# The last token group of a gated state-space mixer, finished in halves, with engines fixed per operation and an order made with an allowance for loads

## The chip, the cores and the metric

The kernel runs on one core of a Trainium2 chip. The metric is the device time of one launch, in microseconds. The core has a matrix engine (TensorE, PE in the profile, with its weight loads as PEld), a vector engine (VectorE, DVE), a scalar engine for tables of functions (ScalarE, ACT) and a queue engine (SyncE, SP), and sixteen DMA engines that both SyncE's and ScalarE's queues feed. Each engine works its own instructions in the order in which they were issued; what depends on another engine waits at a semaphore, and everything behind it on the same engine waits too.

## The reference, cut to what matters

The input is 2048 tokens of 512 channels. It is normalised over the channels, and two branches start from the result xn.

```python
xn = _layernorm(x, axis=-1)
s = _A_ref(xn, ...)          # a long convolution: K from (A, B, C, dt), y = irfft(rfft(K) * rfft(xn)) + xn * Dskip
g = _silu(_B_ref(xn, ...))   # the gate
return x + s * g

# _B_ref: spatial-shift token mixing, then an MLP
h = _gelu(_layernorm(x) @ w1)
hs = concat(shift(h quarters by +1, -1, +2, -2)) @ w2
x1 = x + hs
return x1 + _gelu(_layernorm(x1) @ w3) @ w4        # w3: 512 x 1376, w4: 1376 x 512
```

The convolution kernel K of a channel is a sum over 128 complex modes of a geometric sequence in the token's number. Both K and the convolution run over all 2048 tokens of a channel, so the scan branch needs all tokens before it can give any.

## The kernel before, in words

The tile X holds all tokens in the on-chip memory: 128 partitions x 16 slots x 512 channels, float32. A token group is two slots, 256 tokens; there are eight groups, worked in the order 1, 2, ..., 7, 0 (the list GROUPS). X is overwritten stage by stage: with the normalised input, with x1, with x1 plus the MLP, with its Silu (the gate), with the gate times the scan, and with the final sum.

The stages are these. *params* prepares the modes from A, B, C and dt. *token_mixing* normalises (ln_first), transposes and multiplies by w1 (h_pair, into pb), applies gelu, starts the transform of the tokens (u_stage1), and multiplies the shifted rows by w2 (hs_pair, into pd); on the way the weights w3 and w4 are scaled and split into a high and a low float16 half (prep). *tables* makes the exponentials and waves of all modes (mag, pt) and sums them into K by products into pc. *mlp* multiplies a group's rows by w3 in six blocks (into pb, waiting for x1T, which a DMA transposes), applies gelu into g, splits g into the high and low halves ghl, and accumulates ghl times w4 in pa; the last line of mlp adds the scaled pa to X. *kstage1* and *products* do the transforms of K and the product with the tokens' spectra, for each half of the channels (DH = 256 channels): eight units a half, each of which loads constants (cst), spectra (kin, uin), multiplies, and stores its result (z1e) to a scratch in device memory. *gate* applies Silu to a group, *inverse* loads the scratch (zin), transforms it back and multiplies X by it, and *finish* adds the input (xr, loaded again) and stores the group in four DMAs of 32 partitions.

The groups 1 to 7 take the inverse's result one half of the channels at a time. The last group, 0, keeps the result of both halves in pc (duo[2]) and multiplies by it once, 1024 elements a partition (lines 1238 to 1243).

Each function of ScalarE belongs to a set of tables: exponentials, sine and Silu, gelu, square root, arctangent. A change of set is an instruction of its own (ACT_TABLE_LOAD, issued at line 539).

None of this fixes the order in which instructions are issued. The program first only notes operations, 1751 of them, with what they read and write (Plan.add). Plan.order then walks through time with one clock for each engine and a cost for each operation, and issues them (Plan.issue). At each step it takes the engine that can start next, and on it, of the operations ready within 0.02 us, the one with the lowest value in the table DUE, with a charge for a change of tables (SWITCH) and for a change of TensorE's array mode (KEEP). Work that either VectorE or ScalarE can do (Either: copies, scalings) is offered to both, with a preference by engine (PREFERP, AVOIDP, PREFER, AVOID); a store can go to SyncE's or to ScalarE's queue. A transfer is counted as landed at the time done (lines 515 and 516). Since every instruction is issued by one of two lines, the profile has nearly all of them under L542 (and L539 and L541), and the names of the tiles tell them apart.

The lines that the change touches: release and the choice (464 to 491), the landing of a transfer (515), gate (1223), inverse (1227), finish (1247), mlp (1431 to 1470).

Of the kernel before, what the change touches and what calls it, by code (L numbers as in the profile page):

```python
# [21 lines left out]
D = 512  # L22
# [73 lines left out]
class Op:  # L96
# [17 lines left out]
FIRST, LAND, PAD, LANES = 1.7, 0.45, 0.13, 8  # L114
# [9 lines left out]
SHIFT, KEEP = 0.09, -41.4  # L124
# [159 lines left out]
)  # L284
SWITCH = 196.28
PREFERP, AVOIDP = 150.95, -129.56
PREFER, AVOID = -68.73, 92.63

# [48 lines left out]
class Plan:  # L337
# [115 lines left out]
    def order(self):  # L453
# [10 lines left out]
        def release(op):  # L464
            for e in op.alts:
                pools[e].append(op)
# [1092 lines left out]
```

## Time and profile before

| what | value |
|---|---|
| median of 3 runs | 549.91 us (548.17 to 551.24) |
| profiled execution | 550.05 us, span 548.3 us |
| granted TensorE clock, mean | 0.987 |
| TensorE busy | 524.2 us, 6058 products |
| VectorE busy | 443.2 us, 730 instructions |
| ScalarE busy | 401.5 us, 587 instructions, of them 51 table loads of 1.28 us |
| moved by DMA | 107.33 MB |

The span is the time from the first to the last instruction on the core; the profiled execution's own time has 1.75 us beside it. Busy is the time in which an engine works an instruction; a transfer that is issued counts for the DMA engines and not for the engine that issued it. In an answer of the trace a bracket after an instruction is the time for which its engine was idle before it, and what ended that. A group of lines "x12" is twelve instructions in a row merged.

### The profile page before, as it was taken

What the parts mean: (1) busy time and instruction counts of PE and PEld (TensorE: products, weight loads), DVE (VectorE), ACT (ScalarE), POOL (GpSimd) and SP (SyncE); (2) the same over time, 40 slices, a digit from 0 to 9 for tenths busy, and PEclk for the clock granted to TensorE, in tenths of its full rate; (3) what the DMA queues carried; (4) which work ended last, traced back from release to release, by engine and by line L of the source; (5) the groups of instructions that cost most, each with busy time, mean ns of one, the idle gap of its engine ahead of it and who ended that gap; (6) DMA issues with size and microseconds to landing.
All of it is one profiled execution on the core that took longest, in us unless ns stands there. A gap on an engine that the chain in (4) does not pass through costs nothing.

```text
span 548.3 us, 14226 instructions
## 1 busy us (share of the span) xinstructions
PE 524.2 (96%) x6058; PEld 345.9 (63%) x6058; DVE 443.2 (81%) x730; ACT 401.5 (73%) x587; POOL 0.7 (0%) x6
## 2 busy tenths in 40 slices
PE   9789999999999999899999999999999998999992
PEld 9687676876444576458567657576765666466641
DVE  5899999799999999999999989978244353874376
ACT  2899999699997999997999995968345421722511
POOL 0000000000000000000000000000000000000000
PEclk9989999999999999999999999999999999999997
DMA  8974667844666624566434344446898867969977
GB/s 209 222 192 141 232 219 240 281 138 152 217 196 248 133 59 113 141 199 182 139 122 153 96 145 131 124 135 191 213 347 290 287 193 248 280 182 233 327 248 231
DMA packets 86591, 107.33 MB, mean 196 GB/s; under 512 B 31680, under 2 KB 65728, under 8 KB 85632
## 3 DMA queue, kind: packets, MB, share of 16 engines
q1 hardware_dynamic: 85808, 104.46, 63.6%
q10 hardware_dynamic: 720, 1.97, 1.1%
q8 instruction: 47, 0.77, 0.6%
q14 instruction: 16, 0.13, 0.1%
HBM read 64.46 MB, written 37.75 MB: 186 GB/s over the span
## 4 chain that ended last, share of the span: by engine, by line
PE 71%; DVE 11%; DMA 8%; ACT 6%; issue 2%; SPq 1%; DVEq 0%; ACTq 0%
PE pb L542 29%; PE pa L542 18%; PE pd L542 13%; PE pc L542 10%; DVE X L542 3%; DVE pt L542 3%; DMA cst<-c_gp 2%; ACT mag L542 2%; DMA zin<-scr_Zdb 1%; DMA X<-in_A_u_dram 1%; SPq L542 1%; DMA rawA<-in_A_A_re_dram 1%; ACT pt L542 1%; DVE ghl L542 1%; ACT L539 1%
## 5 line engine op out<-in xcount | busy, mean ns | idle before, releaser
L542 PE MATMUL pb<-x1T,w3h 128*128 128x256 f16 (+1 forms) x1056 | 122.9, 273 | 0.4 <-DMA x1T<-x1s 0.4
L542 PE MATMUL pa<-w4h,ghl 128*128 128x512 f16 (+1 forms) x528 | 122.3, 380 | 0.2 <-DVE ghl L542 0.2
L542 PEld LDWEIGHTS <-w3h 128*128 128x128 f16 (+1 forms) x1056 | 102.8, 100 | 26.7 <-issue 10.8
L542 PEld LDWEIGHTS <-ghl 128*128 128x128 f16 (+1 forms) x528 | 49.3, 98 | 61.8 <-issue 8.7
L539 ACT ACT_TABLE_LOAD x51 | 65.4, 1283 | 8.8 <-DMA out_dram<-X 7.3
L542 ACT ACTIVATE pt<-pt 128x2048 f32<-128x2048 int32 x32 | 60.7, 1906 | 2.0 <-DVE pt L542 1.9
L542 PE MATMUL pb<-xT,w 128*128 128x256 f32 x256 | 59.1, 383 | 1.1 <-ACT xT L542 1.1
L542 DVE TENSOR_TENSOR pt<-mag,pt 128x1024 f32<-128x1024 f32 x48 | 57.5, 1217 | 1.2 <-ACT pt L542 1.1
L542 DVE SCALAR_TENSOR_TENSOR ghl<-g,wsc,ghl 128x512 f16<-128x512 f32 (+1 forms) x48 | 33.4, 701 | 30.9 <-ACT ghl L542 30.6
L542 PE MATMUL pd<-w,hT 128*128 128x512 f32 x116 | 53.1, 599 | 1.4 <-DVE X L542 1.4
L542 PEld LDWEIGHTS pb<-xT,w 128*128 128x128 f32 x256 | 47.2, 190 | 10.7 <-issue 2.7
L542 ACT ACTIVATE g<-pb,wsc 128x512 f32<-128x512 f32 (+1 forms) x48 | 30.5, 649 | 27.3 <-PE pb L542 26.3
L542 ACT ACTIVATE ghl<-g,wsc 128x512 f16<-128x512 f32 (+1 forms) x38 | 26.0, 689 | 28.1 <-PE pa L542 28.0
L542 ACT ACTIVATE mag<-par 128x128 f32<-128x128 f32 x160 | 41.0, 454 | 2.8 <-DMA is<-c_is 2.6
L542 PEld LDWEIGHTS pd<-w,hT 128*128 128x128 f32 x116 | 21.3, 190 | 27.4 <-issue 24.2
L542 DVE TENSOR_TENSOR pt<-pt 128x2048 f32<-128x2048 f32 x16 | 36.4, 2283 | 0.2 <-ACT pt L542 0.2
L542 DVE TENSOR_TENSOR pr<-pd,uin 128x1024 f32<-128x1024 f32 x16 | 19.3, 1221 | 20.3 <-PE pd L542 20.3
L542 PEld LDWEIGHTS pc<-pt 128*32 128x32 f32 x2048 | 29.7, 110 | 9.2 <-issue 8.7
L542 PE MATMUL pc<-pt 128*32 128x64 f32 x2048 | 33.0, 220 | 0.7 <-issue 0.7
L542 ACT ACTIVATE pt<-pt,halfpi 128x2048 f32<-128x2048 f32 x16 | 32.0, 2000 | 0.2
L542 ACT COPY z1e<-pc 128x1024 f32<-128x1024 f32 x7 | 7.1, 1013 | 22.6 <-PE pc L542 22.6
L542 DVE TENSOR_TENSOR pt<-par,ev 128x1024 int32<-128x1024 f32 x16 | 19.5, 1216 | 4.2 <-PE pc L542 4.2
(155 smaller groups left out, 760.2 us busy)
## 6 DMA issues: line engine op xcount, KB each, us to landing
wst<-in_B_w_dram SPq DMA_DIRECT2D x20, 512.0 KB, 4.2
scr_Ud<-ue SPq DMA_DIRECT2D x16, 512.0 KB, 3.3
uin<-scr_Ud SPq DMA_DIRECT2D x32, 256.0 KB, 4.2
cst<-c_gp SPq DMA_DIRECT2D x16, 384.0 KB, 4.6
scr_Uh<-uh SPq DMA_DIRECT2D x8, 512.0 KB, 3.4
scr_Kfa<-k1e SPq DMA_DIRECT2D x8, 512.0 KB, 3.3
kin<-scr_Kfa SPq DMA_DIRECT2D x16, 256.0 KB, 3.0
scr_Zda<-z1e SPq DMA_DIRECT2D x8, 512.0 KB, 5.6
```

Source lines behind the costliest of these rows:

```text
L539: self.engines["ACT"].preload_act_table_set(SETS[table])
L542: ins = [getattr(self.engines[op.eng], name)(*args, **kw).ins for name, args, kw in op.calls]
```

## The change

Three things change together.

First, the last token group is finished in two halves of one slot each (new function pieces). The scaled addition of pa at the end of mlp, the Silu of gate, the product of inverse, the addition of finish: each is done for one slot and then for the other, 512 elements a partition where it was 1024, and each half is stored by four DMAs of its own, eight in all. Before the scaled addition of this group, ScalarE is given a Silu of one element that reads the last gelu's result and writes a scratch element (warm), so that the table of Silu is asked for there.

Second, each operation that two engines can do has its engine fixed by a table of bits (PIN, one for each of now 1760 operations: 1 is VectorE, or SyncE for a store; 0 is ScalarE). The four preferences are gone.

Third, the order is made by other rules: an operation that isn't ready yet can be chosen too, with a charge (WAIT) for each microsecond that it would be waited for; the charges for tables and array mode have other values; the planner counts a transfer as landed MARGIN = 0.6 us later when it decides when its readers are ready (its DMA lanes are freed as before); and the table DUE is new throughout.

```diff
-FIRST, LAND, PAD, LANES = 1.7, 0.45, 0.13, 8
+FIRST, LAND, MARGIN, PAD, LANES = 1.7, 0.45, 0.6, 0.13, 8
-SHIFT, KEEP = 0.09, -41.4
+SHIFT = 0.09
...
-SWITCH = 196.28
-PREFERP, AVOIDP = 150.95, -129.56
-PREFER, AVOID = -68.73, 92.63
+SWITCH, KEEP, WAIT = 35.498, -5.69, 93.442
+PIN = (
+    "10111111111111111111111111111111111111111110111101111111100111111101101111111111111010010010010110011111111111"
...
         def release(op):
-            for e in op.alts:
-                pools[e].append(op)
+            e = min(op.alts)
+            if len(op.alts) > 1 and PIN[op.idx] == "1":
+                e = max(op.alts)
+            pools[e].append(op)
...
             for o in pools[e]:
-                if o.ready <= t + 0.02:
-                    v = o.vt
...
+                v = o.vt + WAIT * max(0.0, o.ready - t)
+                if e == "ACT" and o.table and o.table != table:
+                    v += SWITCH
+                if e == "PE" and o.mode != mode:
+                    v += KEEP
+                if pick is None or (v, o.idx) < score:
+                    pick, score = o, (v, o.idx)
+            pools[e].remove(pick)
             pick.eng = e
+            t = max(t, pick.ready)
...
                 landed.append(done)
+                done += MARGIN
...
     def gate(g):
-        X2 = X[:, 2 * g : 2 * g + 2]
-        A.activation(X2, X2, AF.Silu)
+        for x, _ in pieces(g):
+            A.activation(X[:, x], X[:, x], AF.Silu)
...
         if g == GROUPS[-1]:
             if hf == 0:
                 return
-            ch, py = slice(0, D), pair
+            for x, k in pieces(g):
+                V.tensor_mul(X[:, x], X[:, x], pair[:, k])
+            return
...
-        X2 = X[:, 2 * g : 2 * g + 2]
-        V.tensor_add(X2, X2, xr[q][:, 2 * (g % 2) : 2 * (g % 2) + 2])
-        for r in range(4):
-            E.store(ov[ORDER[r]][:, 2 * g : 2 * g + 2], X2[32 * r : 32 * r + 32])
+        for x, k in pieces(g):
+            V.tensor_add(X[:, x], X[:, x], xr[q][:, 2 * (g % 2) : 2 * (g % 2) + 2][:, k])
+            for r in range(4):
+                E.store(ov[ORDER[r]][:, x], X[32 * r : 32 * r + 32, x])
...
+    def pieces(g):
+        if g != GROUPS[-1]:
+            return [(slice(2 * g, 2 * g + 2), slice(0, 2))]
+        return [(2 * g + k, k) for k in range(2)]
...
-        X2 = X[:, 2 * g : 2 * g + 2]
-        V.scalar_tensor_tensor(X2, duo[0], a4, X2, op0=ALU.mult, op1=ALU.add)
+        if g == GROUPS[-1]:
+            A.activation(warm[:fr], g32[:fr, 0, 0:1], AF.Silu)
+        for x, k in pieces(g):
+            V.scalar_tensor_tensor(X[:, x], duo[0][:, k], a4, X[:, x], op0=ALU.mult, op1=ALU.add)
```

The values of DUE are in units of the planner's own. The ones that the prediction names are counted to their place: the first normalised rows on ScalarE have about -1605, the exponentials of the same time -360 to -280; the last products into pa have -1214 and -1236, the last scan product of group 7 has -713.

More of the change, by code (lines that the diff above doesn't have):

```diff
@@ L131 @@
 DUE = (
[152 rows of a table removed]
-)
-SWITCH = 196.28
-PREFERP, AVOIDP = 150.95, -129.56
-PREFER, AVOID = -68.73, 92.63
[142 rows of a table added]
+)
+SWITCH, KEEP, WAIT = 35.498, -5.69, 93.442
+PIN = (
+    "10111111111111111111111111111111111111111110111101111111100111111101101111111111111010010010010110011111111111"
+    "11111111100010101101101010111111111111111111111111111111111111010110110101011111111111111111111111110000111011"
+    "01101111101111110110101111111111111111111111111101111111111011011111111101101101010111111111111111111111111111"
+    "10111011011010111110111101101110111111111111110101010101010101010101011111111111111111111111111011111111111111"
+    "11111111111111111111111111111111101101111111111111111111111111111011011111111111111111111111111111111111111110"
+    "11011111111111111111111101101101111111101111101111101111101111101111101111101111101001100110100000000011111100"
+    "01111111101111111000111111111111111100011111111011111110001111111101010000000001111110001111111101111111000111"
+    "11111011111110001111111101111111000111111110111001111101111110011110110011110111111001111001111100111110011111"
+    "00111001100111101111110011110011111111001110011111011110011111111011111101111111011111101111111111111101111111"
+    "01111110111111101111110111111101111110111111101111111111111111111110101000000000111111000111111110111111100011"
+    "11111101111111000111111110111111100011111111010100000000011111100011111111011111110001111111101111111000111111"
+    "11111111110001111111101110111111001111100111101111111101111110011110011111001111100111110011100110011110011111"
+    "01111100111110111111011111100111001111111101111110011110111111011111100111110111110111011110111111011111001111"
+    "10011111011111100111101111111101111110011110011111001111100111110011111001111100111100110111111111011100111111"
+    "11001111111111110111111111111111111111110111111111110111111111110111111111110111111111110111111111110100000000"
+    "01111111111111111111111111111111111111111111111111111100101111111111010111010111110110111011111111111011011010"
+)
 class Clock:
@@ L477, in order @@
             for o in pools[e]:
-                if o.ready <= t + 0.02:
-                    v = o.vt
-                    if e == "ACT" and o.table and o.table != table:
-                        v += SWITCH
-                    if e == "PE" and o.mode != mode:
-                        v += KEEP
-                    if len(o.alts) > 1:
-                        on = (PREFERP, AVOIDP) if o.psum else (PREFER, AVOID)
-                        v += on[e != "DVE"]
-                    if pick is None or (v, o.idx) < score:
-                        pick, score = o, (v, o.idx)
-            for k in pick.alts:
-                pools[k].remove(pick)
+                v = o.vt + WAIT * max(0.0, o.ready - t)
[6 more added lines that the diff above has]
+            pools[e].remove(pick)
             pick.eng = e
+            t = max(t, pick.ready)
             pick.cost, pick.calls = pick.alts[e]
```

294 rows, old and new, of the table DUE are left out of this document.

## The prediction

> **What bounds the kernel now.** I read the page first, for the busy shares and the chain of waits, then the busy times by stage, then the idle times of TensorE, and last the order of instructions behind the end of its work. The lines of the page:
>
> ```profile
> span 548.3 us, 14226 instructions
> PE 524.2 (96%) x6058; PEld 345.9 (63%) x6058; DVE 443.2 (81%) x730; ACT 401.5 (73%) x587; POOL 0.7 (0%) x6
> ...
> PE 71%; DVE 11%; DMA 8%; ACT 6%; issue 2%; SPq 1%; DVEq 0%; ACTq 0%
> ```
>
> TensorE is busy for 96% of the span and makes 71% of the chain that ended last. So a change of order can gain only what TensorE idles, what it fills with idle products at the start, and what lies behind its last product. The stages, cut where the kernel changes character (columns: window, its length, then busy time and instruction count of each engine, granted clock, DMA share, GB/s):
>
> ```profile
> 0.00:38.88 38.88, 32.36 (x248) 31.69 (x248) 29.93 (x83) 26.03 (x69) 0.70 (x6) 0.91 0.90 220
> 38.88:130.00 91.12, 91.12 (x814) 67.66 (x814) 84.35 (x180) 84.33 (x113) 0.00 (x0) 1.00 0.60 198
> 130.00:230.00 100.00, 96.68 (x1188) 52.24 (x1184) 99.60 (x170) 95.13 (x157) 0.00 (x0) 1.00 0.54 155
> 230.00:350.00 120.00, 119.33 (x1770) 79.39 (x1767) 116.41 (x169) 109.32 (x149) 0.00 (x0) 1.00 0.48 149
> 350.00:440.00 90.00, 89.64 (x999) 55.78 (x997) 50.14 (x58) 52.17 (x60) 0.00 (x0) 1.00 0.74 234
> 440.00:500.00 60.00, 56.68 (x610) 37.17 (x607) 37.28 (x44) 20.23 (x25) 0.00 (x0) 1.00 0.77 227
> 500.00:536.27 36.27, 36.27 (x391) 21.08 (x398) 18.31 (x24) 11.98 (x15) 0.00 (x0) 1.00 0.94 269
> 536.27:548.30 12.03, 2.12 (x64) 0.91 (x64) 7.13 (x8) 2.34 (x2) 0.00 (x0) 0.70 0.79 239
> ```
>
> Three things are to be seen. Between 38.88 and 536.27 TensorE idles 100.00 - 96.68 = 3.32, then 0.67, 0.36 and 3.32 us, together 7.67. From 130 to 350 VectorE is as full as TensorE (99.60 of 100, 116.41 of 120), and after 350 it is little over half busy. And the last 12.03 us hold almost no products: they are the tail.
>
> The idle times themselves, in the order of time (in brackets the idle time and what ended it):
>
> ```profile
> 154.60 7.13 PE L542 MATMUL pd<-w,hT 128*128 128x512 f32 x16 [0.42 <-DVE X L542]
> 228.41 0.70 PE L542 MATMUL pc<-ksl,kk 32*128 32x512 f32 x2 [1.64 <-ACT k1e L542]
> 356.52 3.67 PE L542 MATMUL pb<-x1T,w3h 128*128 128x256 f16 x32 [0.36 <-DMA x1T<-x1s]
> 457.51 1.10 PE L542 MATMUL pd<-kin,cst 64*32 64x256 f32 x32 [2.00 <-DMA cst<-c_gp]
> 472.85 1.10 PE L542 MATMUL pd<-kin,cst 64*32 64x256 f32 x32 [1.32 <-DMA cst<-c_gp]
> ```
>
> Before 350 VectorE and ScalarE let TensorE wait; after 350 only transfers do, 0.36 + 2.00 + 1.32 = 3.68 us.
>
> The tail, instruction by instruction (start, duration; x7 with SPq or ACTq are DMA issues):
>
> ```profile
> 530.91 5.36 PE L542 MATMUL pa<-w4h,ghl 128*128 128x512 f16 x24
> 531.37 6.14 ACTq L542 DMA_DIRECT2D out_dram<-X  x7
> 536.30 1.28 DVE L542 SCALAR_TENSOR_TENSOR X<-pa,wsc,X 128x1024 f32<-128x1024 f32 x1
> 537.50 0.68 DVE L542 TENSOR_TENSOR X<-X,pc 128x512 f32<-128x512 f32 x1
> 537.82 1.28 ACT L539 ACT_TABLE_LOAD   x1 [7.26 <-DMA out_dram<-X]
> 538.10 0.68 DVE L542 TENSOR_TENSOR X<-X,pd 128x512 f32<-128x512 f32 x1
> 538.70 2.35 DVE L542 TENSOR_TENSOR X<-X,xr 128x1024 f32<-128x1024 f32 x2
> 539.12 1.06 ACT L542 ACTIVATE X<-X 128x1024 f32<-128x1024 f32 x1
> 540.97 1.21 DVE L542 TENSOR_TENSOR X<-X,pc 128x1024 f32<-128x1024 f32 x1
> 542.21 1.22 DVE L542 TENSOR_TENSOR X<-X,xr 128x1024 f32<-128x1024 f32 x1
> ...
> DMA to landing us min/median/max: 2.0/3.3/4.2
> ```
>
> The last products end at 530.91 + 5.36 = 536.27. Then come the scaled addition, the table, the Silu, the product with the scan's result, the addition of the input and the stores, one behind the other on one token group; 542.21 + 1.22 = 543.43 is the end of the arithmetic, and 4.87 us of stores follow. The table load stands behind seven store issues on ScalarE's queue, and it delays the Silu from about 537.7 to 539.12. But VectorE has no gap from 536.30 to 543.43 either: 3.47 us of work for other groups (537.50 to 540.97) is in its row. So the tail has two limits of nearly one length.
>
> **The sum, part by part.** It is made against the profiled execution, 550.05 us: span 548.3 and 1.75 around it. That is 0.14 above the median of 549.91.
>
> *The tail in halves, with the early table.* For half a group I take 0.74 for the scaled addition, 0.66 for the Silu, 0.68 for each product and addition, from the nearest rows of 128x512:
>
> ```profile
> 25.98 0.66 ACT L542 ACTIVATE mag<-mag 128x512 f32<-128x512 f32 x1
> ...
> 529.46 0.74 DVE L542 SCALAR_TENSOR_TENSOR ghl<-g,wsc,ghl 128x512 f16<-128x512 f32 x1
> ```
>
> On a VectorE without other work the scaled additions run 536.30 to 537.7, the first Silu 537.2 to 537.9, the second to 538.6, and the products and additions end at about 540.4 (second Silu, then 0.1, 0.68, 0.68, with the first half's addition between): 3.0 us before 543.43. With all 3.47 us of other work in the way, VectorE remains the limit and gains nothing; three more instructions cost it some 0.2. Counted to their places in the new table of due values, the last scan product of the other groups (due -713) still stands behind the last products into pa (-1214 and -1236), so one group's product and addition, 0.68 + 1.22 = 1.9 us, probably stay behind 536.27. That gives a gain between 3.0 - 1.9 = 1.1 and 3.0; I take 2.0. The one-element Silu waits for the last group's last gelu; behind it on ScalarE stand the remaining scalings into ghl, stores and the two Silus. Its cover is ScalarE's idle time, 36.27 - 11.98 = 24.3 us from 500 on. If a gelu came behind it, two more loads, 2.56 us, would be paid, and the products of the last group would wait for them.
>
> The stores become eight of 64 KB, two by each queue for each half (read off the table of pins). They add four issues, which the first half's lead hides but for one. The last landing is bounded by 2.0 and 3.3 of the row above, against 3.3 now: gain 0 to 1.3, I take 0.5. **Tail: -2.5, between -4.3 and +0.2.**
>
> [...]
>
> *An allowance for each load.* The planner now counts each transfer as landed 0.6 us later when it decides what follows. Nothing is added on the chip. A stall of TensorE behind a load shrinks by at most the allowance if other products stand in the row: 0.36 + 0.6 + 0.6 = 1.56. What is late next is the moved product's own evacuation, on engines that are half idle after 350. Bounds: nothing, and all 3.68. **Loads: -1.6.**
>
> *Engines fixed.* I compared the pins with the engines before, operation by operation. Before 350 us 14 evacuations or scalings leave VectorE and 5 come to it; after 350 it is 4 and 20. From 130 to 350 those are 3 + 2 ghl, 2 x1s and 1 x1n off, 1 ghl and 1 x1s on, priced by these rows:
>
> ```profile
> L542 ACT ACTIVATE ghl<-g,wsc 128x512 f16<-128x512 f32 x32 | 22.9, 723 | 23.6 <-PE pa L542 23.6
> ...
> L542 DVE TENSOR_SCALAR ghl<-g,wsc 128x512 f16<-128x512 f32 x8 | 3.9, 482 | 0.3 <-PE pa L542 0.2
> ...
> L542 DVE TENSOR_SCALAR x1n<-X,rs,bs 128x512 f32<-128x512 f32 x6 | 3.3, 542 | 0.1
> ...
> L542 DVE CAST x1s<-x1n 128x512 f16<-128x512 f32 x3 | 1.3, 418 | 0.0
> ...
> L542 DVE TENSOR_SCALAR ghl<-g,wsc 96x256 f16<-96x256 f32 x2 | 0.7, 347 | 2.2 <-ACT g L542 2.2
> ```
>
> Net 2 x 0.48 + 2 x 0.35 + 0.42 + 0.54 = 2.6 us less on VectorE, where it is full, and about 1.5 times that (723 against 482), 3.9, more on ScalarE, which idles 4.9 + 10.7 us there. TensorE idles 3.99 us in this stage, so at best 2.6 come back; at worst ScalarE's extra 3.9 is what TensorE waits for. I take **-0.7**, nearer to nothing, since much of that idle time hangs on single results and not on the engine's load.
>
> *The start.* With the new due values the first normalised rows (-1605) are the most urgent work on ScalarE; the exponentials beside them have -360 to -280. Before, they stood behind eight exponentials:
>
> ```profile
> 31.48 2.13 ACT L542 ACTIVATE mag<-par 128x128 f32<-128x128 f32 x8
> ...
> 32.86 0.14 DVE L542 SCALAR_TENSOR_TENSOR bs<-mv,rs 128x2 f32<-128x2 f32 x1
> ...
> 33.73 0.81 ACT L542 ACTIVATE X<-X,bs,rs 128x512 f32<-128x512 f32 x1
> ```
>
> Their input was there at 33.00, so 0.73 is to be had; I take **-0.5**. All loads of this stage are reordered too, with the DMA at a share of 0.90; I bound that by +2 and -3, against 38.88 us of which TensorE needs little.
>
> The rest of the order is new as well (due values, the charge for a table, the charge for waiting), which no row prices. Sum: 2.5 + 1.6 + 0.7 + 0.5 = 5.3; 550.05 - 5.3 = 544.75, say **544.8 us**.
>
> **The rivals.**
>
> *The new order closes most of what is open.* For it: 7.67 us of idle TensorE and a start that no engine fills. Against it: each idle time has its own cause, and VectorE stays full to 350. With the whole tail (4.3) and three quarters of the idle time (5.7): 550.05 - 10 = 540.
>
> *The tail is VectorE's, not the table's.* VectorE's unbroken 7.13 us speak for it; its idle 36.27 - 18.31 = 18 us just before speak against it, as there the work would fit. Then the tail gains nothing, and if the loads keep their stalls, only the pins are left: 550.05 - 0.7 = 549.4.
>
> *The early table isn't early.* If the one-element Silu lands behind stores that wait, as the load did, 1.3 us of the tail come back: 546.1.
>
> *Slower: planned waits stand in TensorE's row.* Before, an operation was chosen only if ready within 0.02 us; now each us of waiting costs 93 due units, and a product with a lower due value can be put ahead of one that is ready. On the chip the row is kept: a late load then holds everything behind it. The place is the second half's eight units between 440 and 502, where two late loads cost 3.32, 1.66 each, with the DMA at 0.77 to 0.94. If the other six stall alike: +10.0, and with a 2.5 better tail 557.5. It decides from five such waits more, 8.3 us, which outweigh 5.3 and the 2.75 of measurement. Against it: the allowance works the other way.
>
> **How the numbers follow.** Forecast 0.46 (its own range 541.5 to 548), larger gain 0.22, VectorE's tail 0.15, late table 0.07, slower 0.10. What a measurement of this kernel can tell from no change is about 0.5%, here 547.2 to 552.7. Faster: 0.44 + 0.22 + 0.05 = 0.71; same: 0.02 + 0.15 + 0.02 = 0.19; slower 0.10. The range takes in VectorE's tail and most of the larger gain, with 2 us for the start's upper bound: 538.5 to 552.
>
> **What would show it.** Tail: a table load before the last scaled addition, two Silus of some 0.6 us, and from the last product to the end of the span 9.5 us where 12.03 were. Loads: TensorE's idle time behind cst and x1T together near 2 us where 3.68 were. Pins: VectorE busy 2 to 3 us less between 130 and 350, with less than 3.99 us of idle TensorE. Start: first product of xT near 38.4. The forecast is wrong if TensorE's busy time itself moves by more than 3 us, if the start moves by more than 1, or if new load waits turn up in 440 to 500.

## The result, and the profile after

The changed kernel takes 553.37 us (median of 9 runs, 552.16 to 555.64) where the kernel before takes 548.89 beside it (9 runs, 547.25 to 551.24): a ratio of 1.0081, 95% interval 1.0059 to 1.0104. It is 0.8% slower. The forecast was 544.8, and the time lies above the range of 538.5 to 552.

The profiled execution took 552.2 us. From its page, the span, the busy shares and the chain of waits:

```profile
span 550.2 us, 14225 instructions
PE 527.3 (96%) x6056; PEld 346.1 (63%) x6056; DVE 454.7 (83%) x740; ACT 393.1 (71%) x580; POOL 0.7 (0%) x6
...
PE 83%; DVE 10%; DMA 2%; issue 1%; ACT 1%; SPq 1%
```

TensorE's records show 6056 products where 6058 were, and it is busy 3.1 us longer (527.3 against 524.2); the DMA engines' part of the chain fell from 8% to 2%. The busy times by stage, in the same columns as for the kernel before. The first and the last cut lie at the same places of the work (the first product of xT, the end of the last product into pa), the others at the same times:

```profile
0.00:37.07 37.07, 32.15 (x246) 31.13 (x247) 28.51 (x81) 26.11 (x69) 0.70 (x6) 0.95 0.92 230
37.07:130.00 92.93, 92.93 (x845) 68.61 (x846) 84.72 (x177) 84.55 (x112) 0.00 (x0) 1.00 0.60 197
130.00:230.00 100.00, 93.72 (x1115) 50.38 (x1114) 95.62 (x153) 90.66 (x158) 0.00 (x0) 0.97 0.50 149
230.00:350.00 120.00, 119.84 (x1665) 79.66 (x1668) 117.62 (x168) 115.32 (x155) 0.00 (x0) 1.00 0.49 149
350.00:440.00 90.00, 90.00 (x1133) 56.62 (x1118) 61.14 (x82) 43.94 (x48) 0.00 (x0) 1.00 0.72 226
440.00:500.00 60.00, 60.00 (x657) 40.23 (x655) 40.04 (x49) 18.16 (x22) 0.00 (x0) 1.00 0.80 244
500.00:537.23 37.23, 37.23 (x388) 18.67 (x379) 21.30 (x27) 13.06 (x17) 0.00 (x0) 1.00 0.99 273
537.23:550.20 12.97, 1.46 (x49) 0.75 (x48) 5.72 (x8) 1.26 (x2) 0.00 (x0) 0.66 0.70 193
```

From 350 to 537.23 TensorE has no idle time any more (90.00 + 60.00 + 37.23, all busy): the waits for loads are gone. The trouble is the row from 130 to 230, with 6.28 us of idle TensorE and a clock of 0.97 where every such row had 1.00. The idle times in it, in the order of time:

```profile
135.65 3.31 PE L547 MATMUL pc<-pt 128*32 128x64 f32 x120 [2.81 <-DVE pt L547]
148.37 7.13 PE L547 MATMUL pd<-w,hT 128*128 128x512 f32 x16 [0.29 <-DVE X L547]
156.89 3.70 PE L547 MATMUL pd<-w,hT 128*128 128x512 f32 x8 [0.37 <-DVE X L547]
176.57 7.13 PE L547 MATMUL pd<-w,hT 128*128 128x512 f32 x16 [0.29 <-DVE X L547]
217.22 9.18 PE L547 MATMUL pa<-w4h,ghl 128*128 128x512 f16 x34 [2.38 <-DVE ghl L547]
```

Two stalls are new, 2.81 and 2.38 us, both behind VectorE. That engine is the fullest beside TensorE here, yet it stands still itself a few us before each of them:

```profile
127.97 0.16 DVE L547 TENSOR_SCALAR wsc<-pd 128x1 f32<-128x1 f32 x1 [4.02 <-PE pd L547]
...
210.97 0.75 DVE L547 SCALAR_TENSOR_TENSOR ghl<-g,wsc,ghl 128x512 f16<-128x512 f32 x1 [2.16 <-PE pd L547]
```

Both wait for TensorE's products into pd. The first reads one number a partition, the result of the one-column products pd<-m,ones, and those ended long before:

```profile
121.17 0.38 PE L547 MATMUL pd<-m,ones 1*128 1x1 f32 x2
...
124.34 3.60 PE L547 MATMUL pd<-w,hT 128*128 128x512 f32 x8
```

The result was there at 121.55, and VectorE idles from 123.95 to 127.97: it starts 0.03 us after the end of the eight products (124.34 + 3.60 = 127.94). These write the other half of pd, another bank in the planner's count. In the new order they are issued just ahead of the scaling; in the kernel before the scaling came first. The planner keeps its dependences by bank, and its list for the scaling has the one-column products alone; the compiled program waited for the last product issued into the tile, to 127.94 and not 121.55. The second case is of the same kind: the sum into ghl touches no byte that the products issued ahead of it read, but their tile hw lies in the memory of the ghl ring, and the compiled wait is for the last product that reads hw: the sum starts at 210.97, 0.04 us after the end of the products pd<-w,hw of 209.91 (209.91 + 1.02 = 210.93).

Behind each stall the granted clock fell as well, from 1.00 to 0.50 (last three columns: clock, DMA share, GB/s):

```profile
134.00:136.00 2.00, 0.35 (x16) 0.35 (x20) 2.00 (x3) 2.00 (x5) 0.00 (x0) 0.83 0.00 1
136.00:138.00 2.00, 2.00 (x85) 2.00 (x80) 2.00 (x4) 2.00 (x4) 0.00 (x0) 0.50 0.24 86
138.00:140.00 2.00, 2.00 (x75) 1.37 (x65) 1.36 (x3) 2.00 (x9) 0.00 (x0) 0.82 0.45 184
```

That lacks 2.00 x (0.17 + 0.50 + 0.18) = 1.7 us at full clock, so 3.4 us ran at 0.50. The last 0.3 us of the stall are among these, which leaves a loss of about 1.5 us. The same happened from 216 to 222: 0.81, 0.50 and 0.84 in windows of 2 us, 1.7 us again.

The tail, from the end of the last product into pa at 533.17 + 4.06 = 537.23:

```profile
523.83 1.28 ACT L544 ACT_TABLE_LOAD   x1
525.12 0.20 ACT L547 ACTIVATE warm<-g 96x1 f32<-96x1 f32 x1
...
533.17 4.06 PE L547 MATMUL pa<-w4h,ghl 128*128 128x512 f16 x18
537.27 0.75 DVE L547 SCALAR_TENSOR_TENSOR X<-pa,wsc,X 128x512 f32<-128x512 f32 x1 [0.57 <-PE pa L547]
538.05 0.63 ACT L547 ACTIVATE X<-X 128x512 f32<-128x512 f32 x1 [6.16 <-DVE X L547]
539.31 0.63 ACT L547 ACTIVATE X<-X 128x512 f32<-128x512 f32 x1 [0.63 <-DVE X L547]
539.91 1.83 DVE L547 TENSOR_TENSOR X<-X,xr 128x512 f32<-128x512 f32 x2
540.68 3.25 ACTq L547 DMA_DIRECT2D out_dram<-X  x6
542.37 0.69 DVE L547 TENSOR_TENSOR X<-X,xr 128x512 f32<-128x512 f32 x1
```

The table comes early, the Silus take 0.63, and the arithmetic ends at 543.06, 5.83 after the last product into pa where it was 7.16. But 7.14 us of stores follow where there were 4.87, so that the tail is 12.97 us where it was 12.03.

### The profile page after: what moved, and what is told of

The parts are those of the page before. It is cut to its first block, busy times and chain, and to the rows that moved or that the text cites. A ratio compares the mean times of both kernels' runs of the same rounds, so it can differ in the third digit from the quotient of the medians.

```text
span 550.2 us, 14225 instructions
## 1 busy us (share of the span) xinstructions
PE 527.3 (96%) x6056; PEld 346.1 (63%) x6056; DVE 454.7 (83%) x740; ACT 393.1 (71%) x580; POOL 0.7 (0%) x6
## 4 chain that ended last, share of the span: by engine, by line
PE 83%; DVE 10%; DMA 2%; issue 1%; ACT 1%; SPq 1%
PE pb L547 31%; PE pa L547 23%; PE pd L547 14%; PE pc L547 13%; DVE pt L547 5%; DVE X L547 2%; PE pc L546 1%; DMA rawA<-in_A_A_re_dram 1%; DMA rawA<-in_A_A_im_dram 1%; ACT mag L547 1%; SPq L547 1%; DVE stats L547 1%; DVE w3h L547 1%; DVE w4h L547 1%; PE pd L546 1%
## 5 line engine op out<-in xcount | busy, mean ns | idle before, releaser
L547 PEld LDWEIGHTS pc<-pt 128*32 128x32 f32 x2048 | 31.1, 114 | 10.1 <-DVE pt L547 3.4
L547 ACT ACTIVATE ghl<-g,wsc 128x512 f16<-128x512 f32 (+1 forms) x32 | 21.3, 672 | 22.3 <-PE pa L547 18.8
L547 PE MATMUL pc<-pt 128*32 128x64 f32 x2048 | 34.2, 225 | 3.0 <-DVE pt L547 2.8
L547 DVE BATCH_NORM_STATS2 stats<-X 128x6 f32<-128x512 f32 x32 | 21.1, 678 | 0.0
L547 DVE TENSOR_TENSOR pr<-pr 128x512 f32<-128x512 f32 x32 | 20.9, 684 | 0.2
```

The lines of the kernel that those rows point to most:

```text
L547: ins = [getattr(self.engines[op.eng], name)(*args, **kw).ins for name, args, kw in op.calls]
```

## The experiments

Most of the kernels keep the changed kernel's order (or, where it says so, the order of the kernel before) and move single operations in the list that the planner has made, by a few lines ahead of the issue:

```python
for a, b in MOVED:      # issue a just ahead of b
    out.remove(at[a])
    out.insert(out.index(at[b]), at[a])
```

The runs of the kernel before that stand beside them differ a little (547.92 us for 1 to 4, 548.86 for 5 to 8, 547.67 for 9 to 11), so times are compared as ratios to it, which use all runs and not the medians alone; one per cent is 5.5 us. Beside the medians a second measure helps, since each trace has it exactly: the stretch from the first product of xT to the end of the last product into pa, and the tail from there to the end of the span. A trace is one execution, though: that of 3 is the slowest of its kernel (553.84 us), that of 7 the fastest (546.18).

| kernel | ratio to before, 95% interval | first xT | stretch | tail |
|---|---|---|---|---|
| before | 1 | 38.88 | 497.39 | 12.03 |
| changed | 1.0081 [1.0059, 1.0104] | 37.07 | 500.16 | 12.97 |
| 1 scale first | 1.0019 [1.0004, 1.0033] | 37.33 | 496.16 | 12.91 |
| 2 ghl first | 1.0038 [1.0023, 1.0052] | 37.35 | 496.84 | 12.81 |
| 3 stores shared | 1.0072 [1.0048, 1.0096] | 38.95 | 500.64 | 12.21 |
| 4 idle products | 1.0102 [1.0082, 1.0122] | 37.79 | 500.04 | 13.07 |
| 5 three moves | 0.9944 [0.9923, 0.9965] | 39.12 | 493.22 | 12.26 |
| 6 before, late scale | 1.0119 [1.0085, 1.0152] | 36.81 | 502.41 | 11.98 |
| 7 before, halves | 1.0004 [0.9982, 1.0027] | 37.37 | 494.10 | 12.83 |
| 8 four stores less | 0.9905 [0.9874, 0.9936] | 37.59 | 493.38 | 10.83 |
| 9 before, loads used later | 0.9986 [0.9968, 1.0004] | 38.44 | 495.00 | 12.36 |
| 10 whole group | 0.9961 [0.9944, 0.9979] | 38.84 | 493.07 | 11.99 |
| 11 three moves again | 0.9962 [0.9943, 0.9980] | 37.79 | 492.09 | 12.62 |

**1. The scaling ahead of the products into the other half of pd.**

```diff
+MOVED = ((415, 428),)    # wsc<-pd ahead of the eight products pd<-w,hT
```

> The changed kernel with one operation moved: VectorE's scaling that makes wsc out of the one-column product in pd is issued before the eight products into pd that stand just ahead of it in the changed kernel's order; each engine keeps its own order. Theory (the scaling waits for products into the other half of pd that it doesn't read): VectorE's idle 4.02 us ahead of it goes, with it TensorE's 2.81 us at 135.65 and the 3.4 us at half clock behind it, worth 1.7: 4.5 us less than the changed kernel, 553.4 - 4.5 = 549, between 548 and 550.5. Rival (VectorE is simply full in this stage, and the wait only moves): no change, 552.5 to 554.

Measured: 548.39 us, a ratio of 1.0019 where the changed kernel had 1.0081, so about 3.4 us less by the ratios, and 4.0 less in the stretch. VectorE's and TensorE's rows at the place:

```profile
124.13 0.15 DVE L547 TENSOR_SCALAR wsc<-pd 128x1 f32<-128x1 f32 x1
...
124.60 3.60 PE L547 MATMUL pd<-w,hT 128*128 128x512 f32 x8
...
132.78 1.99 PE L547 MATMUL pc<-pt 128*32 128x64 f32 x128
```

The scaling now runs at 124.13, ahead of the eight products and without idle time, and the products pc<-pt that stood for 2.81 us have none either. The clock is 1.00 from 122 to 140. The first stall was the false wait; the rival, a VectorE that is simply full, is out.

**2. The sum into ghl ahead of the products that read hw.**

```diff
+MOVED = ((826, 555),)    # ghl<-g,wsc,ghl ahead of pd<-w,hw
```

> The changed kernel with one operation moved: VectorE's scaled sum into the second half of ghl is issued before the products that read hw, which stand just ahead of it and lie in the same ring of memory. Theory (it waits for a product whose bytes it doesn't touch): the 2.16 us ahead of it on VectorE and TensorE's 2.38 us at 217.22 go, and the half clock behind it (1.7): 4.1 less, 549.3, between 548.8 and 551 because the third of those products now waits for the sum instead. Rival (VectorE is full and TensorE waits for the next result on it): no change, 552.5 to 554.

Measured: 549.64 us, 1.0038, so 2.4 us less by the ratios and 3.3 by the stretch. The sum starts at 209.31, and pa runs on from 214.83 without the 2.38 us:

```profile
209.31 0.73 DVE L547 SCALAR_TENSOR_TENSOR ghl<-g,wsc,ghl 128x512 f16<-128x512 f32 x1
...
214.83 5.42 PE L547 MATMUL pa<-w4h,ghl 128*128 128x512 f16 x23
```

The mechanism is as expected; the size by the ratios is below the 4.1, at the edge of the wider bound (551 is 2.4 less than 553.4).

**3. Three stores of the end on the other queue.** The stores of the changed kernel from 543 us on (nanoseconds of one issue, first and last start), and what SyncE's queue waited for from 536 on (us in all, times, the longest):

```profile
L547 SPq DMA_DIRECT2D out_dram<-X x9: 314/421/466, 543.6 to 547.3; - x9
L547 ACTq DMA_DIRECT2D out_dram<-X x2: 321/380/438, 543.1 to 543.5; - x2
```

```profile
SPq L547 <- DMA out_dram<-X: 6.0, 2, 3.3
```

SyncE issues nine stores one behind the other, after a wait of 3.3 us for the landing of earlier ones, while ScalarE's queue has none left after 543.5. In the changed kernel's trace the stores of both queues take turns on eight landing semaphores, so a store on one queue can wait for one that the other queue issued late: SyncE's store of 543.58 has the semaphore of ScalarE's store of 541.04, which landed at 543.57.

```diff
+MOVED = ((1719, 1751), (1710, 1751), (1746, 1751))
+ON_ACT = (1719, 1710, 1746)    # three 128 KB stores of earlier groups, to ScalarE's queue
```

> The changed kernel with three 128 KB stores of the end moved from SyncE's queue to ScalarE's, ahead of the last token group's stores. Theory (SyncE's queue is behind: its store waits for a landing that ScalarE's queue gave late, and nine stores follow one by one): with 0.45 us for each issue and 2.2 to its landing the last landing comes 2.9 us earlier: 550.5, between 549.5 and 551.5, and from the last product into pa to the end of the span about 10 us where 12.97 were. Rival (the DMA engines themselves set the end, at 39% and 28% of their time in the last 15 us): no change, 552.5 to 554.

Measured: 551.55 us, 1.0072; against 1.0081 that can't be told from no change. The tail is 12.21 us where it was 12.97, a gain of 0.8 and not 2.9. With both queues at work the DMA engines are nearly full to the end (the tail's windows of this kernel; share and GB/s are the last two columns):

```profile
541.80:543.80 2.00, 0.00 (x0) 0.00 (x0) 1.97 (x3) 0.51 (x1) 0.00 (x0) 1.00 0.97 264
543.80:545.80 2.00, 0.00 (x0) 0.00 (x0) 1.59 (x3) 0.00 (x0) 0.00 (x0) 0.61 0.97 279
545.80:547.80 2.00, 0.00 (x0) 0.00 (x0) 0.00 (x0) 0.00 (x0) 0.00 (x0) 0.50 0.97 246
547.80:549.80 2.00, 0.00 (x0) 0.00 (x0) 0.00 (x0) 0.00 (x0) 0.00 (x0) 0.50 0.89 266
```

So the queue's backlog explains a part of the lost tail, and what lies under it is the rate of the DMA engines.

**4. Idle products in the first stall** (products whose results nothing reads).

```diff
+FILLED = ((724, 10),)    # ten idle products ahead of pc<-pt
```

> The changed kernel with ten idle products (0.22 us each, 2.2 in all) ahead of the products pc<-pt that run into the first stall; nothing else is moved. They stand in the stall's own time. Theory (the granted clock falls because TensorE stood still): the clock of 136 to 138 us stays 1.00 where it was 0.50, and 1.7 us less, 551.7; the stall is still there, shorter by the idle products. Rival (the clock falls for another reason, or the loss isn't on the path): the same 553.4 within 0.5.

Measured: 552.9 us, 1.0102 [1.0082, 1.0122], not less than the changed kernel. The clock did stay up:

```profile
134.00:136.00 2.00, 1.78 (x22) 1.50 (x21) 2.00 (x3) 2.00 (x7) 0.00 (x0) 1.00 0.12 42
136.00:138.00 2.00, 1.62 (x116) 1.62 (x120) 2.00 (x3) 2.00 (x3) 0.00 (x0) 1.00 0.00 0
```

Its idle times that no other engine ended:

```profile
261.36 0.86 PE L547 MATMUL pc<-pt 128*32 128x64 f32 x44 [0.33 <-issue]
...
370.55 0.32 PE L547 MATMUL pc<-pt 128*32 128x64 f32 x7 [0.52 <-issue]
```

Counted from each trace's first product of xT, the work is 1.4 us further than in the changed kernel right behind the stall (the products pa<-uin,cst at 138.19 here and at 138.90 there), and 1.1 us at 155. By 382 all but 0.1 of that is lost again; the two idle times above, 0.33 and 0.52, which the profile puts down to issue, are most of it. That it was the standing still that lowered the clock here is shown (0.50 from 136 to 138 behind the stall, 1.00 with the idle products); that keeping the clock up is worth anything in the end is not, and whether the new idle times come from the 40 more instructions stays open.

**5. The three moves together**, and once more as run 11.

```diff
+MOVED = ((415, 428), (826, 555), (1719, 1751), (1710, 1751), (1746, 1751))
+ON_ACT = (1719, 1710, 1746)
```

> The changed kernel with all three moves: the scaling into wsc ahead of the products into the other half of pd, the sum into ghl ahead of the products that read hw, and three stores of the end on ScalarE's queue. If the three are separate, their gains add: 552.4 - 4.0 - 2.7 - 0.8 = 544.9 where the kernel before has 547.9, a ratio of 0.9945, between 0.991 and 0.997; TensorE then has no idle time over 1 us from its first product of xT to its last into pa. Rival (the second stall is only where VectorE's lack of time shows, and comes back elsewhere): no better than the first move alone, a ratio of 1.000 to 1.003.

Measured: 545.99 us against 548.86, a ratio of 0.9944; once more (run 11), 545.44 against 547.67, 0.9962. The gains add, and the kernel is faster than both. No idle time of TensorE over 0.58 us is left between the first product of xT and the last into pa.

> The three moves together once more, beside the other two on one chip: a ratio of 0.9944 to the kernel before, between 0.992 and 0.9965; the first product of xT somewhere between 36.8 and 39.2, as in the traces so far of either order, and no wait of TensorE for cst over 0.2 us.

Measured: the 0.9962 above, at the upper end of the range. The first product of xT comes at 37.79, and no wait of TensorE for cst is seen.

**6. The false wait put into the kernel before.** Its second group of products into pd goes ahead of the first, and so ahead of the scaling.

```diff
+MOVED = ((428, 415),)    # in the kernel before
```

> The kernel before with the false wait of the changed one put into it: its second group of eight products into pd is issued just ahead of VectorE's scaling into wsc, which TensorE then does ahead of the first group; each other engine keeps its order, and TensorE's differs by this exchange. Theory (that wait is what costs the changed kernel its first stall): VectorE stands for some 3.4 us, the length of those products, and TensorE behind it; 2 to 4.5 us more than the kernel before, 549.9 to 552.4, a ratio of 1.004 to 1.008. Rival (the new order of the loads and pins makes the stall): within 0.002 of the kernel before.

Measured: 555.83 us, 1.0119, by the ratio 6.5 us slower: more than expected, and in the expected sense. VectorE stands for 6.12 us and not 3.4, ScalarE behind it for 5.67 (to 131.63), and TensorE, behind ScalarE, loses 1.50 and 2.79 and then clock:

```profile
126.78 0.16 DVE L542 TENSOR_SCALAR wsc<-pd 128x1 f32<-128x1 f32 x1 [6.12 <-PE pd L542]
...
134.24 1.99 PE L542 MATMUL pc<-pt 128*32 128x64 f32 x128 [1.50 <-ACT kev L542]
139.03 1.10 PE L542 MATMUL pa<-uin,cst 64*32 64x256 f32 x32 [2.79 <-ACT uh L542]
```

The windows behind that:

```profile
140.00:142.00 2.00, 2.00 (x11) 0.97 (x4) 2.00 (x4) 1.98 (x3) 0.00 (x0) 0.63 0.80 269
142.00:144.00 2.00, 2.00 (x3) 0.68 (x2) 2.00 (x4) 1.99 (x2) 0.00 (x0) 0.52 0.74 215
```

One exchange of two operations, with the old engines, the old loads and no halves, costs the kernel before as much as the whole change or more (1.0119 against 1.0081; the intervals overlap).

**7. The halves alone.** The kernel before with pieces, the one-element Silu, and the last group's halves as the most urgent work.

```diff
+DUE = (
+    DUE[:1518] + (-7000.0,) * 3 + DUE[1519:1647] + (-7000.0,) * 2 + DUE[1648:1694] + (-7000.0,) * 2
+    + DUE[1695:1746] + ((-7000.0,) + DUE[1747:1751]) * 2
+)
```

> The kernel before with one part of the change alone: the last token group finished in two halves, and the one-element Silu for its table. TensorE's order is that of the kernel before, its engines are chosen as before; the last group's halves are the most urgent work of VectorE and ScalarE. By the prediction's term for the tail: 2.5 us less, between 4.3 less and 0.2 more, a ratio of 0.9954 (0.992 to 1.0004). Rival (the DMA engines, at 0.88 to 0.99 of their time over the last 12 us, set the end, so that an earlier end of the arithmetic only makes stores wait): within 0.5 us, a ratio of 0.999 to 1.001.

Measured: 548.95 us, 1.0004 [0.9982, 1.0027]: no change. The table is early (520.83), and VectorE has work without a gap all the same, from 531.51 to 538.78, 7.27 us where it had 7.13:

```profile
531.51 1.41 DVE L546 SCALAR_TENSOR_TENSOR X<-pa,wsc,X 128x512 f32<-128x512 f32 x2
532.83 0.68 DVE L546 TENSOR_TENSOR X<-X,pc 128x512 f32<-128x512 f32 x1
533.43 0.68 DVE L546 TENSOR_TENSOR X<-X,pd 128x512 f32<-128x512 f32 x1
534.02 1.22 DVE L546 TENSOR_TENSOR X<-X,xr 128x1024 f32<-128x1024 f32 x1
535.16 1.28 DVE L546 TENSOR_TENSOR X<-X,pc 128x512 f32<-128x512 f32 x2
536.36 2.42 DVE L546 TENSOR_TENSOR X<-X,xr 128x512 f32<-128x512 f32 x3
```

So the arithmetic doesn't end sooner: 538.78 is 7.31 us after the last product into pa (531.47), where it was 7.16. The rival's case, an earlier end that only makes stores wait, did not arise here, and this run can't tell VectorE's limit from that of the DMA engines.

**8. Four stores less.** The three moves, and one earlier group's four stores left out.

```diff
+LEFT_OUT = (1746, 1747, 1748, 1749)    # the four stores of group 1
```

> The three moves, and the four 128 KB stores of one earlier token group left out, so that its rows of the output are not written: 512 KB less to move in the last 30 us, at 265 GB/s 1.9 us of all DMA engines. Theory (once both queues feed them, the DMA engines set the end): 1 to 2 us less than with the three moves alone, and the time from the last product into pa to the end of the span shorter by as much. Rival (the arithmetic's end and the landing of the last stores set it): within 0.5 us of the three moves.

Measured: 543.86 us, 0.9905 where the three moves had 0.9944 (545.99 us, beside the same runs of the kernel before): 2.1 us less, with intervals that still overlap a little ([0.9874, 0.9936] and [0.9923, 0.9965]). The tail is 10.83 us where it was 12.26, the stretch the same within 0.2. The work that was taken away lies well ahead of the last stores, and the end comes sooner. Four issues and their turns on the landing semaphores go with the bytes, so this run alone doesn't separate the two; the DMA engines at 0.97 nearly to the end in experiment 3 speak for the bytes as what sets the tail, once the queues keep up.

**9. Loads used later, in the kernel before.**

```diff
+MOVED = ((1444, 1572), (1434, 1596))    # in the kernel before: other products ahead of pd<-kin,cst
```

> The kernel before with two of TensorE's operations moved, which is what the allowance does: a group of twelve products into pb, 1.31 us, is issued ahead of the products pd<-kin,cst that waited at 457.51, and a group into pa, 1.30 us, ahead of those at 472.85; every other engine and every load keep their order. The two waits were 2.00 and 1.32 us in the first trace of the kernel before, 1.12 and 0.75, and 0.17 and 0.23, in two kernels that have its order there. Theory (the prediction's term of 1.6 for the loads): each wait shrinks by up to 1.3, so 0.4 to 2.6 us less by the run, on the median 1 to 2, a ratio of 0.996 to 0.998, and no wait for cst over 0.7 in 440 to 500. Rival (a wait that is taken away here comes back at the next product of the unit, since the loads themselves are late): a ratio of 0.9985 to 1.0015.

Measured: 546.92 us, 0.9986 [0.9968, 1.0004]. No wait for cst over 0.15 us is left in the trace. In time it is 0.8 us less, inside the rival's range at its edge; the interval holds both no change and the theory's weaker end. The stretch doesn't help, since this trace has 1.40 us of idle time put down to issue at 285.43.

**10. The last group whole.** The three moves with the halves undone.

```diff
-        return [(2 * g + k, k) for k in range(2)]
+        return [(slice(2 * g, 2 * g + 2), slice(0, 2))]
```

> The three moves together, but the last token group finished whole as in the kernel before: one scaled sum, Silu, product, addition and four 128 KB stores where there were two of each and eight of 64 KB. The one-element Silu stays early, and TensorE's order is the same. By the prediction's term (2.0 of the tail's gain is the halves' and the early table's): 1 to 2 us more than the three moves alone, a ratio to the kernel before of 0.996 to 0.998 where they had 0.9944. Rival (the end is set by what the DMA engines have to store, which halves don't change): the same as the three moves within 0.7 us, 0.993 to 0.9957.

Measured: 545.35 us, 0.9961, beside 0.9962 for the three moves run with it (11). The number alone fits the theory's range, which started from 0.9944; against the run beside it, it is the rival's "the same". The halves are worth nothing here either. The arithmetic ends 6.06 us after the last product into pa, with halves 5.83: of the 1.33 that the changed kernel gains there, 0.23 is the halves', and the rest is that less of the other groups' work stands behind.

## Why the prediction was wrong, by its own steps

The forecast was 5.3 us less than the profiled 550.05; measured were 4.5 more between the medians. The two false waits account for most of the 9.8 between: the three moves bring the ratio from 1.0081 to 0.9944 and 0.9962, 1.2 to 1.4%, 6.5 to 7.5 us, of which the stores are at most 0.8. The tail's 2.5, which never came, is most of the rest, and half of the loads' 1.6 and the start's 0.5 go with it.

**"The rest of the order is new as well (due values, the charge for a table, the charge for waiting), which no row prices."** This is the step that failed. An unpriced part was entered at nothing, in the sum and in the range's upper end alike. Its bounds could not have been zero: every re-made order puts other neighbours side by side, and what the compiled program waits for beyond the planner's dependences is then left to chance. The kernel before had such an exchange within a few instructions, and its price is 6.5 us (experiment 6). Which of the new values put these neighbours together isn't shown. One of the prediction's own signs of error pointed there: TensorE's busy time moved by 3.1 us, over the 3 that were named, as the clock of 0.50 behind the two stalls made the products longer, by some 1.5 and 1.7 us.

**Engines fixed, -0.7.** The count was right: VectorE is busy 95.62 + 117.62 = 213.24 us from 130 to 350 where it was 216.01, 2.8 less, and 2.6 was forecast. By operations it is as counted too (ghl 9 to 5, x1n 4 to 3, x1s 2 to 1); that the busy times agree so closely is partly luck, since the stalls also push other work past 350. The conclusion wasn't right. TensorE's idle time there is 6.28 + 0.16 = 6.44 where it was 3.99, because VectorE stood still for results; its load was not the limit. "Much of that idle time hangs on single results and not on the engine's load" was said of the kernel before, and not turned on the new order.

**Loads, -1.6.** The mechanism was right: in the trace of the changed kernel, and in all eight of the others in its order, no wait for cst is over 0.16 us. The size rested on one execution. In the three traces that have the order of before at these places (before, experiments 6 and 7), the two waits together were 3.32, 1.87 and 0.40 us. Alone it measured 0.8 us, with an interval from 1.8 less to 0.2 more.

**The tail, -2.5.** The table, the two Silus and the earlier end of the arithmetic came as described, the last by 1.33 us. The failed step is "four issues, which the first half's lead hides but for one" together with a last landing bounded by the landing times of single stores. Nine stores stood in SyncE's queue, and behind the queue stood the DMA engines' rate (a share of 0.97 from 541.8 to 547.8 in experiment 3). The prediction named two limits of the tail, and this third one could be read in the kernel before: from 536 to 546 its DMA engines were at shares of 0.88 to 0.98. The forecast 9.5 us from the last product to the end measured 12.97. The rival that the tail is VectorE's describes the halves alone (experiment 7): VectorE works without a gap, and the tail gains nothing (1.0004). That its 549.4, which holds the pins' 0.7, lies near the 548.95 measured there is chance.

**The table loads, 1.28 us each.** The prediction priced two more of them at 2.56 us, the loads' own time and nothing behind them. In the changed kernel that price holds: the load at 523.83 takes 1.28 us, and the one-element Silu starts at 525.12, 0.01 behind its end; behind none of the 49 loads of this trace does ScalarE stand for more than 0.13 us.

**The start, -0.5.** 37.07 against 38.88 looks like a gain of 1.8, over the 1 that was named as a sign of error. It is neither. The first product of xT comes at 38.88, 36.81, 37.37 and 38.44 us in the order of before, and between 37.07 and 39.12 in the nine traces of the new one. These times go with the granted clock of the start: the five latest, 38.44 to 39.12 (before, experiments 3, 5, 9 and 10), are the five traces whose clock averages 0.91 up to there, and the eight with 0.95 or 1.00 have 36.81 to 37.79. At 1.00 the order of before has 36.81 and 37.37 and the new one 37.33 to 37.79 (four traces), so nothing of the 0.5 shows. Whether the slower clock makes the start late, or a later input makes both, isn't shown.

**The slower rival** had a wait in a row that is kept, and a price of the right order, but put it behind late loads in 440 to 500. It came in VectorE's row, at 124 and 209, and no planned wait was in it. Its chance of 0.10 was too low for a part of the change that no row prices.

## What to carry to other kernels

When an order is made anew, look for the neighbours that it creates: a small result read out of a tile whose other half is being written, or two tiles that share memory. The planner's dependences don't have those waits; the compiled program's do, and here moving one instruction ahead of its neighbour was worth 3.4 and 2.4 us, as much as the kernel with all three moves gains over the one before (2.1 to 3.1, experiments 5 and 11). Before a wait or a late start in one profile enters a sum, see whether another execution of the same order has it, and before a tail is shortened by arithmetic, compare the bytes that are still to be stored with the DMA engines' share.

## What the runs showed of the hardware that was not expected

The granted clock of TensorE fell from 1.00 to 0.50 behind idle times of 2.38 to 2.81 us: behind 2.81 and 2.38 in the changed kernel and behind 2.79 in experiment 6, where the windows from 140 to 144 have 0.63 and 0.52. Each time some 3.4 us ran at 0.50. It stayed at 1.00 behind 2.00 (at 457.51 in the kernel before) and 1.64 (228.41). The length of one idle time doesn't decide alone: at the start of the changed kernel the clock fell at about 26 us (0.54 from 26 to 27, 0.50 from 27 to 29), behind idle times of 2.01 and 1.01 with 0.66 us of work between them, and in experiment 1 it stayed at 1.00 behind 1.75 and 1.01. What does decide isn't shown.

The same order shows different waits from execution to execution: the start by 2.1 us (36.81 to 38.88 for the order of before), the two loads by 2.9 (0.40 to 3.32), and TensorE's idle time put down to issue ahead of one group of products pd<-kin,cst from 0.17 (288.94, experiment 6) to 1.40 us (285.43, experiment 9). A median over many runs holds the mean of these; one profile holds one draw.
